# Moving twelve weight loads from the sync queue to GpSimd's queue

## The chip, the core and the metric

The kernel runs on one core of one Trainium2 chip. The metric is the device time of one execution in microseconds (us), the median of several runs. One more execution is recorded by the hardware profiler; its trace is what the tables and rows below are from.

## What is computed

Three layers follow each other. First comes a windowed attention over 2 x 8 heads of 576 positions. Its result, 1152 tokens of 512 numbers, goes through a layer of eight experts, each token to one of them. Last comes a dense layer with a gated activation.

```python
x = attention(q, k, v)                      # window of 64; (1152, 512), float32
e = argmax(x @ w_gate); g = softmax(x @ w_gate)[e]
y = g * (relu(x @ w1[e]) @ w2[e])           # 8 experts, 512 -> 1024 -> 512, float32 weights
h = y @ w_in                                # 512 -> 2048
out = (h * clip(h + 3, 0, 6) / 6) @ w_out   # 2048 -> 512
```

The dense layer's weights `w_in` and `w_out` arrive as float64. The chip reads them as pairs of 32-bit words and the kernel turns them into float32 itself.

## The kernel before

**Stages.** Up to about 67 us of the trace the kernel does attention. From about 67 to 235 us it does the experts ("the expert stage" below), from 235 us to the end the dense layer. The weights of an expert or of the dense layer are cut into units of 256 hidden columns. A unit has two halves of 512 KB, one for each matrix. An expert half is loaded into a `raw` buffer (six of them) by `weights_in` (lines 280 and 283), then split into a high and a low part for three-pass products: ScalarE casts the high part (line 267), VectorE subtracts to get the low part (line 272), both into `wt` buffers (eight). Two of the experts are small ("tiny") and use the `raw` halves without a split. TensorE's products of the weights are line 253.

**The float64 pieces.** A dense unit is converted in four pieces of 512 KB (`conv64`). Each is loaded into a `raw64` buffer, of which there are three (shown as `raw` in the trace), from `w_in` at line 196 or from `w_out` at line 199. Then follow one operation on ScalarE (line 206) and six on VectorE (lines 210, 214, 221, 227, 230 and 236), which go through the scratch tiles `c64` and `t64` (two each, shown as `c` and `t`). The last one, the add at line 236, makes the `raw64` buffer free. The pieces of the first three dense units (`NSC = 3`, twelve pieces) are worked on beside the experts: the float32 result is stored to a DRAM scratch by GpSimd (line 239) and read again for the dense stage at line 1134. The pieces of the later five units are converted in the dense stage and stay on the chip.

**What sets the order.** Each engine and each queue runs its instructions in the order in which they were written. That order is written by a small planner. It keeps an estimated clock for each engine (`est`; "D" stands for the DMA traffic, "P" for GpSimd), and a list of jobs sorted by due time. After every piece of hand-ordered work `fill(limit)` writes further operations of the jobs: one on "D" if it may start by `limit + 4.0`, one on any other engine only if it would end by `limit + 0.5`.

```python
def fill(limit):
    if live[0]:
        while advance(lambda j, e, t, c: t <= limit + SLACK_D if e == "D" else t + c <= limit + SLACK):
            pass
```

A conversion piece is such a job: load, absolute value on ScalarE, six operations on VectorE, and a store on GpSimd where the piece belongs to the first three units (`m is None`). Its load may be written only when the planner knows when a `raw64` buffer is free. GpSimd's own queue holds, in the expert stage, ten gathers of token rows (line 805) and the twelve stores.

In the listing below the sync queue is `nc.sync` and GpSimd's queue `nc.gpsimd`. In the profile they are SPq and POOL or POOLq; DVE is VectorE, ACT is ScalarE, PE is TensorE.

Of the kernel before, what the change touches and what calls it, by code (L numbers as in the profile page):

```python
# [23 lines left out]
def tile_kernel(ctx, tc, q, k, v, w_gate, w1, w2, w_in, w_out, out, cap):  # L24
    nc = tc.nc
    B, H, S, D = q.shape
# [151 lines left out]
    NSC = 3  # L178
# [3 lines left out]
    w_out32 = w_out.bitcast(U32)  # L182
# [3 lines left out]
    def conv64(u, i, dst):  # L186

        box = {}  # L190

        def load():
            box["raw"] = raw = cv.tile([128, 2 * HW], U32, name="raw64", bufs=NR64)
            if i < 2:
                src = w_in32[256 * i : 256 * i + 256, 2 * FU * u : 2 * FU * u + 2 * FU]
                nc.sync.dma_start(raw.rearrange("p (c f) -> p c f", c=2), src.rearrange("(c p) f -> p c f", p=128))
            else:
                r0 = FU * u + 128 * (i - 2)
                nc.sync.dma_start(raw, w_out32[r0 : r0 + 128, :])
            w = raw.rearrange("p (n t) -> p n t", t=2)  # L200
            box["lo"], box["hi"] = w[:, :, 0], w[:, :, 1]

        def c_abs():
            box["c"] = cv.tile([128, HW], U32, name="c64", bufs=NC64)
            box["t"] = cv.tile([128, HW], F32, name="t64", bufs=NC64)
            nc.scalar.activation(box["c"].bitcast(F32), box["hi"].bitcast(F32), AF.Abs)  # L206

        def c_clamp():
            c = box["c"].bitcast(F32)
            nc.vector.tensor_scalar(out=c, in0=c, scalar1=TINY, scalar2=HUGE, op0=ALU.max, op1=ALU.min)  # L210

        def c_shift():
            c = box["c"]
            nc.vector.tensor_scalar(
                out=c, in0=c, scalar1=0x07FFFFFF, scalar2=3, op0=ALU.bitwise_and, op1=ALU.logical_shift_left
            )

        def a_join():
            d = dst()
            box["a"] = a = box["hi"].bitcast(F32) if d is None else d  # L220
            nc.vector.scalar_tensor_tensor(
                out=a.bitcast(U32), in0=box["hi"], scalar=0xC0000000, in1=box["c"],
                op0=ALU.bitwise_and, op1=ALU.bitwise_or,
            )

        def c_power():
            nc.vector.tensor_single_scalar(box["c"], box["a"].bitcast(U32), 0xFF800000, op=ALU.bitwise_and)

        def t_low():
            nc.vector.scalar_tensor_tensor(  # L230
                out=box["t"], in0=box["lo"], scalar=2.0 ** -52, in1=box["c"].bitcast(F32), op0=ALU.mult, op1=ALU.mult
            )

        def t_add():
            a, t = box["a"], box["t"]
            nc.vector.tensor_tensor(out=a if u >= NSC else t, in0=a, in1=t, op=ALU.add)

        def store():
            nc.gpsimd.dma_start(wd_dram[u][:, HW * i : HW * i + HW], box["t"])

        return load, c_abs, c_clamp, c_shift, a_join, c_power, t_low, t_add, store

    NR64, NC64 = 3, 2
# [83 lines left out]
    with ExitStack() as actx:  # L327
# [343 lines left out]
        for j in range(NJ):  # L671
            p = 10 * j + (PRIO["tail"] if j == NJ - 1 else 0)
# [44 lines left out]
        p = 10 * NE + PRIO["top"]  # L717
# [278 lines left out]
        p = -100  # L996
# [57 lines left out]
    for n, (small, b) in enumerate(TEAMS):  # L1054
        at_ = dict.fromkeys("abw", 0)
        order = ORDER[n]
        for c in order:
            f = at_[c]
# [23 lines left out]
    def spend(e, cost, ready=0.0):  # L1082
        est[e] = max(est[e], ready) + cost
        return est[e]
# [16 lines left out]
    r_raw, r_wt, r_64, r_ct = Ring(2 * NRAW), Ring(2 * NWT), Ring(NR64), Ring(NC64)  # L1101
# [16 lines left out]
    def take_raw(m, h):  # L1118
        r_raw.take()
        raw_t[m, h] = rawp.tile([128, HALF], F32, name="raw")  # L1120
# [26 lines left out]
    def conv_job(u, i, m=None):  # L1147
        h = i // 2
        ix = {}

        def dst():
            return None if m is None else raw_t[m, h][:, HW * (i % 2) : HW * (i % 2) + HW]

        load, c_abs, *mid, t_add, store = conv64(u, i, dst)

        def gate_load():
            a = 0.0 if m is None or (m, h) in raw_t else r_raw.free(raw_at[m, h])
            b = r_64.free()
            return None if a is None or b is None else max(a - 2.0, b)

        def run_load(e, fin):
            if m is not None and (m, h) not in raw_t:
                take_raw(m, h)
            ix["raw"] = r_64.take()
            load()
            return fin + 2.0

        def run_abs(e, fin):
            ix["ct"] = r_ct.take()
            c_abs()  # L1170
            return fin

        def plain(fn):
            def run(e, fin):
                fn()
                return fin + 0.13

            return run

        def run_add(e, fin):  # L1180
            t_add()
            r_64.rel[ix["raw"]] = fin
            if m is not None:
                r_ct.rel[ix["ct"]] = fin
                raw_ready[m, i] = fin + 0.2
            return fin + 0.2

        def run_store(e, fin):
            store()
            r_ct.rel[ix["ct"]] = fin + 2.0  # L1190
            stored[u, h] = stored.get((u, h), 0) + 1
            return fin

        now = lambda: 0.0
        ops = [({"D": 1.46}, gate_load, run_load), ({"A": 0.6}, r_ct.free, run_abs)]
        ops += [({"V": c}, now, plain(fn)) for c, fn in zip((0.34, 0.4, 0.62, 0.34, 0.62), mid)]
        ops.append(({"V": 0.62}, now, run_add))
        return ops + ([({"P": 1.1}, now, run_store)] if m is None else [])
# [32 lines left out]
    for m, (kind, s, u) in enumerate(units):  # L1231
        for i in range(NPC):
            if not whole(m):
                add_job(m + 0.1 * i, m, split_job(m, i))
            if kind == "d" and u >= NSC:
                add_job(m - AHEAD[1] + 0.1 * i, m, conv_job(u, i, m))
            elif kind == "d":
                add_job(m + ZDUE + 0.1 * i, m, conv_job(u, i))
        if kind == "e" or u < NSC:
            for h in range(2):  # L1240
                add_job(m - AHEAD[0] + 0.1 * h, m, load_job(m, h))
# [427 lines left out]
    def dense_again():  # L1669

        for t0 in range(0, NTOK, 512):
            n = min(512, NTOK - t0)
            acc = [bank("acc") for _ in range(n // 128)]
            for u in range(DFF // FU):
                halves = [wk.tile([128, 2, NC, 256], F32R, name="xT256", bufs=XTB) for _ in range(2)]
                halves = [x.rearrange("p a c f -> p a (c f)") for x in halves]
                for i in range(NPC):
                    r = wk.tile([128, HW], F32, name="xg", bufs=3)
                    if u < NSC:
                        nc.sync.dma_start(r, wd_dram[u][:, HW * i : HW * i + HW])  # L1680
                    else:
                        load, c_abs, *mid, t_add, _ = conv64(u, i, lambda: r)
                        for fn in (load, c_abs, *mid, t_add):
                            fn()
                    high, low = split_ops(halves[i // 2], r, i % 2)
                    high("A")
                    low()
# [302 lines left out]
```

## Time and profile before

| | |
|---|---|
| median of 3 runs | 446.98 us (444.02 to 447.99) |
| the profiled execution: time, span of its trace | 445.77 us, 444.1 us |
| TensorE busy | 408.7 us, 92% of the span |
| VectorE busy | 321.5 us, 72% |
| ScalarE busy | 225.2 us, 51% |
| GpSimd busy | 57.0 us, 13% |
| DMA traffic | 75.99 MB, mean 171 GB/s |
| mean granted clock of TensorE | 0.978 of full speed |

Busy shares are means over stages that have different limits, so each stage has to be read on its own. DMA share in the windows is the mean busy share of the core's 16 DMA engines; it can exceed 1 slightly.

### The profile page before, as it was taken

The page shows a single profiled execution, that of the slowest core. Times are in us where ns is not written, and L with a number is a line of the kernel's source. Part 1 is how long each engine was busy: PE and PEld are TensorE (multiplying, and loading weights), DVE is VectorE, ACT ScalarE, POOL GpSimd, SP SyncE. Part 2 cuts the span into 40 slices and gives each one's busy share as a digit, 9 for nine tenths or more (in the row PEclk, how much of TensorE's full clock was granted, in tenths as well). Part 3 has the DMA queues.
Part 4 walks back from the last instruction along what each step waited for, and adds up shares of the span by engine and source line. Part 5 has one row for each costly group of instructions (what it writes and reads, how often), then busy time and mean ns, then how long its engine had stood idle before and what let it go on. Part 6 is the DMA issues. An engine that isn't in the chain of part 4 may idle for free.

```text
span 444.1 us, 8559 instructions
## 1 busy us (share of the span) xinstructions
PE 408.7 (92%) x3055; PEld 347.8 (78%) x3055; DVE 321.5 (72%) x865; ACT 225.2 (51%) x494; POOL 57.0 (13%) x120
## 2 busy tenths in 40 slices
PE   7999888797798699999999999999999999999991
PEld 4877665595696699997889998888888888998981
DVE  2888967597799599989967999999999422222430
ACT  4776763552567586744668453455553222322330
POOL 8533403003002100210000000000000000110110
PEclk9999999999699889999999999999999999999997
DMA  9897958939996999939985323442410000110101
GB/s 173 195 226 174 307 193 267 359 126 286 373 376 194 354 311 318 289 96 345 368 295 181 99 90 100 138 124 70 139 50 0 1 0 0 49 47 1 47 27 52
DMA packets 68883, 75.99 MB, mean 171 GB/s; under 512 B 31104, under 2 KB 49536, under 8 KB 68832
## 3 DMA queue, kind: packets, MB, share of 16 engines
q1 hardware_dynamic: 66288, 67.13, 49.4%
q0 software_dynamic: 2544, 8.23, 5.2%
q8 instruction: 26, 0.43, 0.4%
q14 instruction: 25, 0.20, 0.1%
HBM read 67.49 MB, written 7.86 MB: 170 GB/s over the span
## 4 chain that ended last, share of the span: by engine, by line
PE 63%; DMA 14%; DVE 12%; ACT 5%; issue 3%; SPq 1%; POOL 0%; POOLq 0%; ACTq 0%; DVEq 0%
PE banks L253 55%; DMA raw<-in_moe_w_dram 7%; DVE wt L272 3%; DMA raw<-in_moe_w_out_dram 3%; PE banks L628 2%; PE banks L510 2%; DMA c<-x_dram,sidx 1%; ACT wt L267 1%; DMA v_sb<-in_v_dram 1%; DMA k_sb<-in_k_dram 1%; DVE neg L587 1%; PE banks L574 1%; PE banks L1470 1%; PE banks L610 1%; ACT pe L600 1%
## 5 line engine op out<-in xcount | busy, mean ns | idle before, releaser
L253 PE MATMUL banks<-x,wt 128*128 128x320 f32 (+3 forms) x576 | 107.1, 336 | 0.7 <-ACT x L1386 0.4
L253 PEld LDWEIGHTS banks<-x,wt 128*128 128x128 f32 x576 | 94.3, 188 | 10.9 <-DVE wt L272 0.8
L272 DVE TENSOR_TENSOR wt<-raw,wt 128x512 fp32r<-128x512 f32 x128 | 82.9, 685 | 17.6 <-ACT wt L267 17.2
L253 PE MATMUL banks<-wt,g 128*128 128x512 f32 x384 | 92.8, 390 | 0.0
L267 ACT CAST wt<-raw 128x512 fp32r<-128x512 f32 x128 | 74.6, 620 | 29.7 <-DMA raw<-in_moe_w_dram 20.9
L253 PEld LDWEIGHTS banks<-wt,g 128*128 128x128 f32 x384 | 71.6, 188 | 14.2
L1556 ACT ACTIVATE r<-banks,c_three 128x320 f32<-128x320 f32 (+3 forms) x48 | 27.9, 581 | 70.0 <-PE banks L253 70.0
L1559 DVE SCALAR_TENSOR_TENSOR gf<-r,banks 128x320 f32<-128x320 f32 (+3 forms) x48 | 26.5, 552 | 47.6 <-ACT r L1556 47.2
L253 PE MATMUL banks<-xT,wt 128*128 128x256 f32 (+2 forms) x288 | 38.5, 283 | 1.9 <-DVE wt L272 1.7
L253 PEld LDWEIGHTS banks<-xT,wt 128*128 128x128 f32 x288 | 34.9, 191 | 3.9 <-DVE wt L272 1.9
L253 PE MATMUL banks<-h,wt 128*128 128x256 f32 (+2 forms) x288 | 37.0, 279 | 0.0
L253 PEld LDWEIGHTS banks<-h,wt 128*128 128x128 f32 x288 | 34.7, 192 | 0.5 <-issue 0.5
L1562 ACT CAST g<-gf 128x320 fp32r<-128x320 f32 (+2 forms) x40 | 21.4, 535 | 21.1 <-DVE gf L1559 20.9
L253 PE MATMUL banks<-wt,xT 128*128 128x256 f32 x144 | 23.7, 315 | 7.3 <-ACT wt L267 7.1
L1565 DVE TENSOR_TENSOR g<-gf,g 128x320 fp32r<-128x320 f32 (+2 forms) x40 | 23.3, 583 | 9.5 <-ACT g L1562 9.1
L253 PEld LDWEIGHTS banks<-wt,xT 128*128 128x128 f32 x144 | 21.0, 213 | 9.8 <-ACT wt L267 8.4
L206 ACT ACTIVATE c<-raw 128x512 f32<-128x512 f32 x32 | 21.5, 674 | 10.5 <-DVE t L230 10.1
L1602 POOL DMA_INDIRECT out_dram<-raw,cidx x4 | 3.9, 987 | 166.9 <-issue 164.3
L253 PE MATMUL banks<-wt,h 128*128 128x512 f32 x72 | 20.7, 424 | 3.7 <-ACT h L1436 3.7
L587 DVE CUSTOM_DVE_ANT_0 neg<-banks,tmask 128x128 f32<-128x128 f32 x72 | 16.2, 285 | 9.2 <-PE banks L574 9.2
L600 ACT ACTIVATE pe<-neg,nmx 128x128 f32<-128x128 f32 x72 | 22.3, 392 | 0.1
L230 DVE SCALAR_TENSOR_TENSOR t<-raw,c 128x512 f32<-128x512 uint32 x32 | 22.0, 687 | 0.4
(285 smaller groups left out, 566.2 us busy)
## 6 DMA issues: line engine op xcount, KB each, us to landing
raw<-in_moe_w_dram SPq DMA_DIRECT2D x64, 512.0 KB, 6.0
raw<-in_moe_w_in_dram SPq DMA_DIRECT2D x16, 512.0 KB
raw<-in_moe_w_out_dram SPq DMA_DIRECT2D x16, 512.0 KB, 3.9
early<-in_moe_w_dram SPq DMA_DIRECT2D x8, 512.0 KB, 4.5
wd_dram<-t POOLq DMA_DIRECT2D x12, 256.0 KB, 6.2
raw<-wd_dram SPq DMA_DIRECT2D x6, 512.0 KB, 5.5
x_dram<-xt SPq DMA_DIRECT2D x9, 256.0 KB, 4.8
q_sb<-in_q_dram SPq DMA_DIRECT2D x8, 256.0 KB, 4.0
```

Of the source, the lines that this page charges most:

```text
L206: nc.scalar.activation(box["c"].bitcast(F32), box["hi"].bitcast(F32), AF.Abs)
L230: nc.vector.scalar_tensor_tensor(out=box["t"], in0=box["lo"], scalar=2.0 ** -52, in1=box["c"].bitcast(F32), op0=ALU.mult, op1=ALU.mult)
L253: nc.tensor.matmul(out, l, r, start=(start and n == 0), stop=(stop and n == len(pairs) - 1))
L267: nc.scalar.copy(hi, r)
L272: V.tensor_tensor(out=lo, in0=r, in1=hi.bitcast(F32), op=ALU.subtract)
L510: nc.tensor.transpose(pt[:, hp, :], t[:, 2 * hp : 2 * hp + 2, :].rearrange("p h d -> p (h d)"), ident)
L587: V.tensor_tensor_reduce(out=neg[:, hp, :], in0=box["sp", g][:, hp, :], in1=tmask[:, first, :], scale=-1.0, scalar=3.0e38, op0=ALU.add, op ...
L600: nc.scalar.activation(pe[:, hp, :], neg[:, hp, :], AF.Exp, bias=nmx[:, hp : hp + 1], scale=-1.0)
L1556: nc.scalar.activation(r, ph, AF.Relu, bias=c_three)
L1559: V.scalar_tensor_tensor(out=gf, in0=r, scalar=6.0, in1=ph, op0=ALU.min, op1=ALU.mult)
L1562: nc.scalar.copy(hi, gf)
L1565: V.tensor_tensor(out=lo, in0=gf, in1=hi.bitcast(F32), op=ALU.subtract)
```

## The change

The loads of the twelve pieces that are converted beside the experts are issued from GpSimd's queue. The pieces of the dense stage keep the sync queue. The planner's cost of such a load goes to GpSimd ("P", 1.1 us), and the DMA estimate still gets its 1.46 us behind it.

```diff
+        queue = nc.gpsimd if u < NSC else nc.sync
         def load():
...
-                nc.sync.dma_start(raw.rearrange("p (c f) -> p c f", c=2), src.rearrange("(c p) f -> p c f", p=128))
+                queue.dma_start(raw.rearrange("p (c f) -> p c f", c=2), src.rearrange("(c p) f -> p c f", p=128))
             else:
                 r0 = FU * u + 128 * (i - 2)
-                nc.sync.dma_start(raw, w_out32[r0 : r0 + 128, :])
+                queue.dma_start(raw, w_out32[r0 : r0 + 128, :])
...
             ix["raw"] = r_64.take()
             load()
-            return fin + 2.0
+            return (fin if m is not None else spend("D", 1.46, fin)) + 2.0
...
-        ops = [({"D": 1.46}, gate_load, run_load), ({"A": 0.6}, r_ct.free, run_abs)]
+        ops = [({"D": 1.46} if m is not None else {"P": 1.1}, gate_load, run_load), ({"A": 0.6}, r_ct.free, run_abs)]
```

## Rows read from the trace of the kernel before

**Rows 1.** The page: busy time, and the chain that ended last, by line.

```profile
PE 408.7 (92%) x3055; PEld 347.8 (78%) x3055; DVE 321.5 (72%) x865; ACT 225.2 (51%) x494; POOL 57.0 (13%) x120
...
PE banks L253 55%; DMA raw<-in_moe_w_dram 7%; DVE wt L272 3%; DMA raw<-in_moe_w_out_dram 3%; PE banks L628 2%; PE banks L510 2%; DMA c<-x_dram,sidx 1%; ACT wt L267 1%; DMA v_sb<-in_v_dram 1%; DMA k_sb<-in_k_dram 1%; DVE neg L587 1%; PE banks L574 1%; PE banks L1470 1%; PE banks L610 1%; ACT pe L600 1%
```

**Rows 2.** Windows by stage: length, busy times, granted clock, DMA share, GB/s.

```profile
67.00:235.00 168.00, 149.93 (x1153) 129.56 (x1151) 138.79 (x318) 98.02 (x213) 20.21 (x24) 0.96 0.88 291
235.00:330.00 95.00, 94.32 (x480) 82.18 (x481) 89.87 (x177) 49.03 (x91) 0.00 (x0) 1.00 0.37 111
...
76.00:88.00 12.00, 8.75 (x44) 6.09 (x44) 6.79 (x12) 6.34 (x14) 0.00 (x0) 1.00 1.06 362
88.00:153.00 65.00, 53.35 (x427) 47.14 (x425) 53.24 (x127) 35.23 (x77) 10.24 (x12) 0.94 0.86 283
153.00:190.00 37.00, 36.54 (x275) 34.62 (x276) 35.88 (x80) 28.21 (x60) 2.72 (x2) 0.92 0.94 307
190.00:235.00 45.00, 43.99 (x370) 37.23 (x368) 36.50 (x78) 24.80 (x57) 2.91 (x5) 1.00 0.82 276
```

**Rows 3.** Timeline of the sync queue: start, length, line, what it loads.

```profile
82.71 0.98 SPq L196 DMA_DIRECT2D raw<-in_moe_w_in_dram  x2
...
88.73 0.38 SPq L280 DMA_DIRECT2D raw<-in_moe_w_dram  x1
98.34 0.34 SPq L199 DMA_DIRECT2D raw<-in_moe_w_out_dram  x1
...
132.24 0.37 SPq L280 DMA_DIRECT2D raw<-in_moe_w_dram  x1
140.43 0.38 SPq L196 DMA_DIRECT2D raw<-in_moe_w_in_dram  x1
...
185.79 0.37 SPq L280 DMA_DIRECT2D raw<-in_moe_w_dram  x1
195.65 3.36 SPq L199 DMA_DIRECT2D raw<-in_moe_w_out_dram  x2
```

**Rows 4.** Windows around the gaps in rows 3; columns as in rows 2.

```profile
93.00:98.00 5.00, 5.00 (x47) 4.43 (x46) 4.86 (x13) 2.27 (x6) 0.00 (x0) 1.00 0.02 5
...
107.00:114.00 7.00, 0.88 (x8) 0.64 (x6) 1.74 (x5) 0.79 (x2) 0.19 (x1) 0.78 1.05 359
114.00:118.00 4.00, 3.85 (x18) 3.33 (x20) 3.87 (x8) 3.64 (x9) 0.00 (x0) 0.54 1.07 365
...
136.00:141.00 5.00, 4.75 (x34) 3.93 (x34) 4.68 (x10) 4.74 (x11) 0.30 (x1) 1.00 0.30 97
...
149.50:153.30 3.80, 0.05 (x2) 0.01 (x1) 1.21 (x4) 1.92 (x5) 0.00 (x0) 0.80 1.06 309
153.30:157.00 3.70, 3.70 (x11) 3.12 (x12) 3.70 (x9) 3.69 (x8) 0.00 (x0) 0.50 1.03 355
...
190.00:196.00 6.00, 6.00 (x55) 5.28 (x54) 5.70 (x16) 3.00 (x7) 0.09 (x1) 1.00 0.02 5
```

**Rows 5.** Timeline of ScalarE: in brackets the idle time before, and its releaser.

```profile
79.33 0.62 ACT L267 CAST wt<-raw 128x512 fp32r<-128x512 f32 x1 [2.32 <-DMA raw<-in_moe_w_dram]
...
113.48 2.23 ACT L267 CAST wt<-raw 128x512 fp32r<-128x512 f32 x4 [5.30 <-DMA raw<-in_moe_w_dram]
```

**Rows 6.** Groups by line, 67 to 235 us: busy, mean ns, idle before.

```profile
L805 POOL DMA_INDIRECT xg<-x_dram,sidx x10 | 12.0, 1198 | 34.5 <-PE banks L1306 31.9 <-issue 1.7 <-PE banks L1483 0.3
...
L206 ACT ACTIVATE c<-raw 128x512 f32<-128x512 f32 x12 | 8.1, 681 | 0.2 <-DVE top_f L1773 0.2
L239 POOL DMA_DIRECT2D wd_dram<-t x12 | 7.1, 590 | 98.3 <-DVE t L236 67.5 <-DVE ks L1734 24.0 <-ACT y L1456 6.6
```

**Rows 7.** DMA issues of the page: KB each, median us to landing.

```profile
wd_dram<-t POOLq DMA_DIRECT2D x12, 256.0 KB, 6.2
...
xg<-x_dram,sidx POOLq DMA_INDIRECT x10, 6.7
```

**Rows 8.** Timeline of GpSimd, the last of the three gathers before the experts.

```profile
73.31 1.27 POOL L805 DMA_INDIRECT xg<-x_dram,sidx  x1 [0.30 <-issue]
```

## The prediction

> **What bounds the kernel now.** I read the page first. TensorE is busy for 92% of the span, and on the chain that ended last it has most of the time, but a load of expert weights (`raw<-in_moe_w_dram`) stands there with 7% and VectorE's split with 3% [rows 1]. So the chain leaves TensorE for the DMA somewhere. The windows by stage say where [rows 2]: in the dense stage up to 330 us TensorE is busy for 94.3 of 95 us and nothing is to be had. In the expert stage, 67 to 235 us, it is busy for 149.9 of 168. Nearly all that is missing lies in one stretch: from 88 to 153 us it is busy for 53.35 of 65, so it idles 11.65 us there; from 153 to 190 it idles 0.46 and from 190 to 235 us 1.0.
>
> The next view is the timeline of the sync queue [rows 3]. Three times a load of a float64 piece (line 199 or 196) goes out long after the load written before it: 98.34 after 88.73, 140.43 after 132.24, 195.65 after 185.79. The piece needs a `raw64` buffer, and that comes free with the add of an earlier piece on VectorE. Everything behind it on the queue waits too, and that is expert halves. The DMA engines run dry meanwhile: their share is 0.02 from 93 to 98 us, 0.30 from 136 to 141, 0.02 from 190 to 196 [rows 4]. Before the first of these gaps, from 76 to 88 us, the share was 1.06 at 362 GB/s [rows 2]. So it isn't a lack of bandwidth; the traffic is held back by the order of one queue.
>
> TensorE feels it later. From 107 to 114 us it is busy for 0.88 of 7 us, from 149.5 to 153.3 us for 0.05 of 3.8 [rows 4]. The first idle stretch ends when ScalarE casts an expert half at 113.48, after 5.30 us of waiting for that half's DMA [rows 5], which had been queued behind the piece that left at 98.34. TensorE then works with a granted clock of 0.54 from 114 to 118 us and of 0.50 from 153.3 to 157 [rows 4]: after an idle stretch it is granted mostly the lower of its two levels, 1.2 instead of 2.4 GHz. That costs about 3.85 x 0.46 = 1.8 and 3.70 x 0.50 = 1.85 us of work. The third gap costs hardly anything, since TensorE loses only 1.0 us from 190 us on.
>
> **The change, part by part.**
>
> *Removed: twelve loads from the sync queue.* Each took 0.34 to 0.38 us to issue [rows 3], which the queue's idle time hides. What counts is the wait in front of them, which leaves with them. Expert halves then go out as soon as their own `raw` buffers are free. What is late next? Three limits for the stretch of 65 us. TensorE could gain its idle time and the first slow clock, 11.65 + 1.8 = 13.5 us. The DMA moves 283 x 65 = 18.4 MB, which takes 50.8 us at 362 GB/s, so it could give up 14 us. VectorE has 53.24 us of work there; in the next stretch, where nothing was held back, it was busy for 35.88 of 37 us (0.970), and in the dense stage for 89.87 of 95 (0.946) [rows 2]. At 0.970 its work needs 54.9 us and at 0.946 56.3. VectorE is therefore the tightest, and the gain is 8.7 to 10.1 us; I take the middle, 9.4. The third gap adds at most the 1.0 us that TensorE idles after it. The second slow clock (1.85 us) I count only in the lower end of the range, because from 153 us on VectorE is full anyway.
>
> *Added: twelve loads on GpSimd's queue.* No load of this kind is in the trace. The nearest are the stores, 0.590 us of GpSimd each, and the gathers, 1.198 [rows 6]. I take 0.6 for the four-kilobyte rows of `w_out`, which are 128 as in a store, and 1.2 for the pieces of `w_in` with twice as many. Both kinds are six, so it is 6 x 0.6 + 6 x 1.2 = 10.8 us (7 to 14 at the ends) on an engine that is busy for 20.2 of 168 us [rows 2]. That is hidden, and with no cover at all it would be 10.8 us late. From GpSimd a store of 256 KB takes 6.2 us to land and a gather 6.7 [rows 7]; a load of 512 KB should take 6 to 8.
>
> *Added: waits on GpSimd's queue.* The wait for the `raw64` buffer moves there. Behind it stand stores of other pieces and gathers. But the load of piece n+3 and the store of piece n wait for the same add, so the store loses at most one issue, 1.2 us. The gathers have their own long waits there now (one of 31.9 us for TensorE's transposes [rows 6]) and go out a team of experts ahead, except the last one. Cost: 0, at most 1.2 us for that last gather.
>
> *Moved: the first three loads.* Their buffers are free from the start, and GpSimd is free once the third gather is out, at 73.31 + 1.27 = 74.6 us [rows 8]. In the code these loads now follow those gathers as soon as the planner's limit reaches them. Before, they stood behind expert halves and the first two went out at 82.71 us [rows 3]. So 3 x 0.524 MB come into a stretch in which the DMA runs at 362 GB/s, which is 4.3 us of traffic. If all of it goes ahead of expert halves that are awaited, TensorE is 4.3 us late; if none does, 0. That the halves are awaited there is seen at 79.33, where ScalarE's cast waited 2.32 us for one [rows 5]. The two queues share the engines, so I take half, 2.2 us. In exchange VectorE may do a piece in its idle time from 76 to 88 us (5.2 us); I count nothing for it.
>
> *Moved in the code's order.* A load on "P" is written when it would end by `limit + 0.5`, before it could be up to 4 us ahead. On GpSimd's queue only the order counts, and what stands before it is short. Cost 0, with the rival below as its bound.
>
> The Trainium skill's page "DMA: Bandwidth & Descriptors", section "Issuing engines are not separate DMA queues", speaks against the change: transfers from any engine end up on the same 16 DMA engines and interleave, and issuing from several only saves the time of issue. By that the time would stay at 447. The gaps of rows 4 speak for another reading here: the engines stood empty while a queue waited.
>
> Sum: 9.4 + 1.0 - 2.2 = 8.2 us less. The profiled execution took 445.77 us, so it would take 437.6. It lies 1.2 us below the median of the runs shown, 446.98; against that median, which I forecast, it is 438.8.
>
> **The rivals.**
>
> *VectorE or ScalarE takes the place of the wait, about no change.* VectorE was busy for 4.86 of 5 us just while the DMA was empty [rows 4]: it did pieces one after another. If it does so again, and now earlier, the splits of the expert halves stand behind them, the `raw` buffers come free late, and the sync queue waits for those instead. For this: 53.24 of 65 us is not much slack. Against: in the gaps there was no expert half to split at all. Of the 9.4 us perhaps a third would be left, less the 2.2: 1 us, 446.
>
> *ScalarE stands at the absolute value (line 206), slower.* The planner lets it come 1.1 + 1.46 + 2.0 = 4.6 us after the load's turn. If a load takes 6.7 us to land like a gather [rows 7], after 1.2 of issue, ScalarE waits up to 3.3 us for each of the nine later pieces, 30 us in all, and the casts of expert halves stand behind it. ScalarE has 70 of 168 us idle [rows 2], so I let half reach TensorE: 15 - 8.2 = 7 us slower, 454. It decides from the point at which a load lands more than 4.6 us after its buffer is free and VectorE isn't late itself. Against it: twelve such operations waited 0.2 us in all before [rows 6], and they need the store of an earlier piece, which lands after 6.2 us, as late as the load.
>
> The skill has a rule that would make this worse: "SBUF — State Buffer", section "SBUF: two separate sides", says that GpSimd can't write descriptors while VectorE runs an operation in a two-port mode, and that switching to the other queues avoids it. No row here shows such a stall: the stores took 0.59 us each beside a full VectorE.
>
> *It doesn't do what it says.* GpSimd's queue is as much in order as the other one. If loads stand there behind stores (their idle time before is 98.3 us [rows 6]), the pieces come as late as now, the scratch is read late, and the dense stage starts late. Expert halves still flow, so it ends about where it was: 445 to 450, taken as 447.
>
> **How the numbers follow.** The forecast has 0.60, and all of its own range (434 to 442.5) is faster by over 1%; 1% of 447 is 4.5 us, about what a measurement of this kernel can tell from no change. The first rival has 0.18 (no change), the slower one 0.14, the last 0.08, half of it no change and half slower. The forecast gets most because the empty DMA and its cause are seen directly; the rest is large because every engine's order is written anew by the planner. So faster 0.62 (with 0.02 of the first rival), same 0.20, slower 0.18. Low end: all limits at their best, 10.1 + 1.0 + 1.85 and nothing for the first loads, 13 us: 434, and 1 below it for the spread of the runs. High end: no change, and 1.5 us above it.
>
> **What would show it.** Right: from 88 us on no load of an expert half stands behind a piece; the DMA share has no window near 0; the idle time of TensorE at 107 and 149 us and the low clock after it are gone; the dense stage starts about 8 us earlier and is as long as before. Wrong: casts or line 206 on ScalarE that wait for DMA, a late first product at 82 to 88 us, waits of the sync queue for splits (line 272) that grow by as much as those for pieces shrink, or VectorE with new idle time before splits.

## The result and the profile after

The median went from 447.49 us (444.02 to 448.96, four runs) to 441.52 us (440.29 to 443.19, four runs). The ratio is 0.9887, 95% interval 0.9849 to 0.9925: 1.1% faster, 6.0 us by the medians. The profiled execution took 440.54 us (span 438.8), 5.2 us less than that of before; its forecast was 437.6. The changed kernel was timed again later: 440.26 us, ratio 0.9879 (0.9841 to 0.9918). All line numbers from 192 on are two higher than before.

First the page, busy times and chain, to be held against [rows 1].

```profile
PE 407.9 (93%) x3055; PEld 345.7 (79%) x3055; DVE 321.2 (73%) x864; ACT 225.0 (51%) x495; POOL 65.1 (15%) x132
...
PE banks L255 36%; DMA raw<-in_moe_w_in_dram 1%; DVE raw L223 1%; DVE t L232 1%; DVE raw L238 1%; DVE g L1567 1%; DVE c L212 1%; DVE wt L274 1%; DMA wd_dram<-t 1%; DVE gf L1561 0%; DVE c L229 0%; DVE c L216 0%; DVE part L1595 0%; POOL out_dram L1604 0%; ACT c L208 0%
```

This chain can be followed back only to 233.14 us, so its shares say nothing about the expert stage and can't be held against the 7% of before. At its start stand a store to the scratch (`wd_dram<-t`), a load of a float64 piece and the conversion of pieces. What became of the expert stage is seen in the windows. The windows by stage and around the old gaps, with the columns of [rows 2] and [rows 4]:

```profile
76.00:88.00 12.00, 9.54 (x52) 6.62 (x50) 8.42 (x15) 6.44 (x14) 0.00 (x0) 1.00 1.05 362
88.00:153.00 65.00, 63.03 (x506) 56.30 (x506) 59.70 (x141) 44.99 (x100) 11.52 (x14) 1.00 0.96 326
153.00:190.00 37.00, 36.49 (x308) 33.60 (x307) 33.75 (x79) 21.99 (x49) 6.19 (x7) 1.00 0.88 289
190.00:235.00 45.00, 43.93 (x336) 38.50 (x335) 38.97 (x76) 26.91 (x58) 4.03 (x7) 1.00 0.62 213
235.00:330.00 95.00, 89.67 (x423) 75.29 (x422) 84.79 (x167) 46.41 (x84) 0.00 (x0) 0.98 0.39 117
...
93.00:98.00 5.00, 5.00 (x49) 4.47 (x48) 5.00 (x14) 3.79 (x9) 0.60 (x1) 1.00 0.76 223
107.00:114.00 7.00, 6.43 (x48) 5.16 (x47) 6.90 (x14) 5.65 (x12) 0.00 (x0) 1.00 1.04 381
149.50:153.30 3.80, 3.54 (x24) 3.28 (x25) 3.80 (x9) 3.15 (x7) 0.00 (x0) 1.00 1.06 371
190.00:196.00 6.00, 5.62 (x45) 4.87 (x45) 5.93 (x12) 4.26 (x10) 1.15 (x2) 1.00 0.97 277
```

The stretch from 88 to 153 us is as forecast: TensorE is busy for 63.03 us instead of 53.35, the DMA share is 0.96 instead of 0.86, both idle stretches and the low clock after them are gone. But the row of 235 to 330 us has turned: 89.67 of 95 us instead of 94.32. The timeline of TensorE in the changed kernel tells where (in brackets the idle time before, and its releaser):

```profile
221.16 7.01 PE L255 MATMUL banks<-x,wt 128*128 128x320 f32 x46 [0.36 <-ACT x L1388]
...
260.26 3.48 PE L255 MATMUL banks<-wt,g 128*128 128x512 f32 x14 [1.23 <-DVE wt L274]
266.50 5.04 PE L255 MATMUL banks<-x,wt 128*128 128x320 f32 x20 [2.18 <-DVE wt L274]
```

The same mark in the kernel before, TensorE's first long group in the dense layer (in both kernels two products stand 0.93 us ahead of it), and GpSimd's last store:

```profile
235.84 7.01 PE L253 MATMUL banks<-x,wt 128*128 128x320 f32 x46 [0.36 <-ACT x L1386]
...
221.89 0.54 POOL L239 DMA_DIRECT2D wd_dram<-t  x1 [6.61 <-ACT y L1456]
```

So the dense layer starts 14.68 us earlier (235.84 - 221.16), and the span ends only 5.3 us earlier (444.1 - 438.8): 9.4 us come back behind this first dense group. The chain of the changed kernel, in order of time (start, length, what), shows the beginning of it:

```profile
233.14 2.33 DMA wd_dram<-t
235.97 5.62 DMA raw<-in_moe_w_in_dram
241.61 0.67 ACT c L208
```

VectorE's timeline has the wait that this makes:

```profile
242.31 0.43 DVE L212 TENSOR_SCALAR c<-c 128x512 f32<-128x512 f32 x1 [7.81 <-ACT c L208]
```

GpSimd's and the sync queue's timelines belong to it, with the third gather for [rows 8]:

```profile
72.62 1.27 POOL L807 DMA_INDIRECT xg<-x_dram,sidx  x1 [0.30 <-issue]
73.89 1.55 POOL L198 DMA_DIRECT2D raw<-in_moe_w_in_dram  x2
...
233.14 0.54 POOL L241 DMA_DIRECT2D wd_dram<-t  x1 [16.55 <-DVE t L238]
```

```profile
205.99 29.94 SPq L1136 DMA_DIRECT2D raw<-wd_dram  x6
235.97 0.94 SPq L198 DMA_DIRECT2D raw<-in_moe_w_in_dram  x2
```

The twelfth piece is stored at 233.14, 12 us after the first dense group; before it was stored at 221.89, 14 us ahead of it. The last of the six reloads (line 1136) waits for that store, and the pieces of the dense stage stand behind it on the sync queue. ScalarE stands for the first of them until 241.61, and VectorE behind it for 7.81 us. From then on VectorE converts without a pause until 272 us, and TensorE waits for the split at 260.26 and 266.50.

### The profile page after: what moved, and what is told of

It reads as the page before. It is cut to its first block, busy times and chain, and to the rows that moved or that the text cites. A ratio compares the mean times of both kernels' runs of the same rounds, so it can differ in the third digit from the quotient of the medians.

```text
span 438.8 us, 8564 instructions
## 1 busy us (share of the span) xinstructions
PE 407.9 (93%) x3055; PEld 345.7 (79%) x3055; DVE 321.2 (73%) x864; ACT 225.0 (51%) x495; POOL 65.1 (15%) x132
## 5 line engine op out<-in xcount | busy, mean ns | idle before, releaser
L255 PE MATMUL banks<-x,wt 128*128 128x320 f32 (+3 forms) x576 | 108.7, 340 | 2.6 <-DVE wt L274 2.2
L255 PEld LDWEIGHTS banks<-x,wt 128*128 128x128 f32 x576 | 95.8, 191 | 12.8 <-DVE wt L274 2.7
L255 PE MATMUL banks<-wt,g 128*128 128x512 f32 x384 | 94.3, 392 | 3.1 <-DVE wt L274 1.2
L255 PE MATMUL banks<-wt,xT 128*128 128x256 f32 x144 | 21.7, 293 | 1.3 <-DVE wt L274 0.8
L223 DVE SCALAR_TENSOR_TENSOR raw<-raw,c 128x512 uint32<-128x512 uint32 x32 | 22.0, 688 | 0.5
L255 PEld LDWEIGHTS banks<-wt,xT 128*128 128x128 f32 x144 | 18.6, 190 | 3.9 <-DVE wt L274 2.3
```

What stands on the lines that cost most here:

```text
L223: nc.vector.scalar_tensor_tensor(out=a.bitcast(U32), in0=box["hi"], scalar=0xC0000000, in1=box["c"], op0=ALU.bitwise_and, op1=ALU.bitwise_or,)
L255: nc.tensor.matmul(out, l, r, start=(start and n == 0), stop=(stop and n == len(pairs) - 1))
```

## The experiments

The change has two halves, the queue and the planner's costs, and the planner writes every engine's order anew. So the first two kernels separate them, and the next try the end of the chain.

**The queue alone.** The planner is left as it was; PE, VectorE and ScalarE run exactly the order of before. As an edit of the changed kernel:

```diff
-            return (fin if m is not None else spend("D", 1.46, fin)) + 2.0
+            return fin + 2.0
...
-        ops = [({"D": 1.46} if m is not None else {"P": 1.1}, gate_load, run_load), ({"A": 0.6}, r_ct.free, run_abs)]
+        ops = [({"D": 1.46}, gate_load, run_load), ({"A": 0.6}, r_ct.free, run_abs)]
```

> The twelve loads go out from GpSimd's queue, but the planner's costs stay as in the kernel before, so PE, VectorE and ScalarE run the very order of before. Theory (the wait in front of the loads was what cost): the three gaps of the DMA go, and the gain is at least that of the change, 5 to 10 us: 437 to 443 us. Rival (the new order of the engines brought the gain): within 1% of before, 445 to 449.

Measured: 438.63 us (437.31 to 441.89) against 445.25, ratio 0.9856 (0.982 to 0.9892). With no other order on any engine the gain is there, so the wait in front of the pieces was the cause. Its windows, from 88 us and in the dense stage:

```profile
88.00:153.00 65.00, 60.28 (x483) 53.07 (x484) 61.96 (x145) 43.23 (x95) 14.45 (x18) 1.00 0.95 319
...
235.00:330.00 95.00, 94.75 (x468) 81.56 (x467) 90.46 (x177) 46.27 (x83) 0.00 (x0) 1.00 0.32 95
```

VectorE is at 61.96 of 65 (0.953), where the prediction had set its limit (0.946 to 0.970). TensorE's idle time there falls from 11.65 to 4.72 us, and in the three windows in which the DMA had run dry (93 to 98, 136 to 141, 190 to 196 us) its share is 0.75, 0.99 and 1.00. The dense stage is full, as before.

**The planner alone.** The loads stay on the sync queue; PE, VectorE and ScalarE run exactly the order of the changed kernel.

```diff
-        queue = nc.gpsimd if u < NSC else nc.sync
+        queue = nc.sync
```

> The planner's costs as in the changed kernel, so PE, VectorE and ScalarE run the order of after, but all loads stay on the sync queue. Theory (queue): expert halves stand behind pieces again, with gaps of the DMA as before, 446 to 455 us. Rival (order): as fast as the changed kernel, 440 to 443.

Measured: 439.91 us (438.55 to 441.05), ratio 0.9875 (0.9846 to 0.9904). My theory that the gaps would stay fell. The planner's new entry writes a load only if it would end by `limit + 0.5`; before it could be 4 us ahead. So more expert halves stand in front of it. Sync queue and windows of this kernel:

```profile
170.79 0.37 SPq L282 DMA_DIRECT2D raw<-in_moe_w_dram  x1
180.61 2.97 SPq L198 DMA_DIRECT2D raw<-in_moe_w_in_dram  x2
```

```profile
88.00:153.00 65.00, 63.51 (x515) 57.04 (x514) 59.92 (x141) 45.34 (x101) 8.21 (x10) 1.00 0.99 330
...
170.00:181.00 11.00, 11.00 (x98) 10.10 (x97) 10.19 (x24) 6.49 (x16) 0.12 (x1) 1.00 0.33 98
```

Two waits for a `raw64` buffer of the old length are left: 7.0 us before the load at 90.51, behind which the next expert half leaves at 94.01 (in the changed kernel, where no piece stands in front of it on this queue, at 93.98), and 9.4 us before 180.61. During the second TensorE is busy for all of 11 us. Either half removes the gaps that hurt. On this chip the queue alone takes 6.6 us off, the planner alone 5.3, both together 6.0 in the first result, so the gains don't add. This kernel has the new order of every engine besides the later loads; which of the two brought its gain was not taken apart.

**The reloads on GpSimd too.** In the changed kernel the sixth reload held the sync queue until 235.9 us. Here the six reloads leave from GpSimd.

```diff
-                nc.sync.dma_start(t, wd_dram[u][:, HALF * h : HALF * h + HALF])
+                nc.gpsimd.dma_start(t, wd_dram[u][:, HALF * h : HALF * h + HALF])
```

> The changed kernel with the six loads that read the scratch again (line 1136) on GpSimd's queue too; the engines' order is that of after. Theory (in the changed kernel the sixth of them holds up the first float64 pieces of the dense stage on the sync queue until 236 us, and ScalarE, VectorE and then TensorE stand for them from 234 to 270 us): those waits go, 4 to 7 us less than the changed kernel, 434 to 438. Rival (the dense stage is bound by VectorE there anyway): no change, 440 to 443.

Measured: 439.80 us (437.09 to 441.61), ratio 0.9864 (0.9827 to 0.9901), so no clear gain over the changed kernel; 4 to 7 us were expected. Two dense pieces now leave at 208 us, and the absolute value at 235.13 waits for nothing. ScalarE's next cast takes the wait over:

```profile
243.49 0.62 ACT L269 CAST wt<-raw 128x512 fp32r<-128x512 f32 x1 [7.24 <-DMA raw<-wd_dram]
```

GpSimd in the same kernel, the last store and the reload that waits for it to land:

```profile
234.40 0.55 POOL L241 DMA_DIRECT2D wd_dram<-t  x1 [16.54 <-DVE t L238]
239.45 0.54 POOL L1136 DMA_DIRECT2D raw<-wd_dram  x1 [4.51 <-DMA wd_dram<-t]
```

So freeing the sync queue is not enough. What is waited for now is the twelfth piece itself; that an earlier twelfth piece would save the time isn't shown by this run, and the run on its due time below speaks against it.

**All pieces on GpSimd.** The dense stage's twenty loads move too.

```diff
-        queue = nc.gpsimd if u < NSC else nc.sync
+        queue = nc.gpsimd
```

> The changed kernel with the twenty pieces of the dense stage on GpSimd's queue as well. There they stand behind the store of the last piece (233 us) instead of behind the load that reads it again. Theory: the first of them comes only some 2 to 3 us earlier than in the changed kernel, so 1 to 3 us less, 438 to 441. Rival (loads from GpSimd cost more than from the sync queue): slower than the changed kernel, over 443.

Measured: 441.36 us (440.33 to 442.07), ratio 0.9907 (0.988 to 0.9934). This can't be told apart from the changed kernel, and the rival's over 443 us didn't come; TensorE is busy for 89.22 us from 235 to 330. The loads now stand behind the last store (230.84) instead of the sixth reload.

**The changed kernel again**, beside the next three.

> The changed kernel once more, beside the next three on the same chip: 439 to 443 us.

Measured: 440.26 us (438.6 to 442.29) against 445.4.

**The twelve pieces due earlier.** The due time of the twelve scratch pieces is moved forward in the planner's list, so that it finishes them ahead of more of the dense stage's work.

```diff
-    ZDUE = 3
+    ZDUE = -2
```

> The changed kernel with an earlier due time for the twelve pieces (ZDUE -2 instead of 3). VectorE's order for the first eleven stays; the twelfth piece is done after 1 of the dense stage's four VectorE chunks instead of after all 4. Theory (the dense stage is late because the twelfth piece is joined, stored and read again too late in VectorE's order): its store leaves before 225 us instead of at 233, the waits from 234 to 270 us shrink, and the time is 2 to 5 us under the changed kernel's. Rival (VectorE has too much work there in any order): same as the changed kernel.

Measured: 439.59 us (438.49 to 441.65), ratio 0.988 (0.9846 to 0.9914), the same as the changed kernel, where 2 to 5 us less were expected. The last store comes at 225.65 instead of 233.14, and the small waits of the dense stage give way to a single one of the same size:

```profile
235.91 5.45 PE L255 MATMUL banks<-x,wt 128*128 128x320 f32 x20 [4.72 <-DVE wt L274]
```

VectorE's wait has only moved, it is no shorter (8.26 us instead of 7.81):

```profile
234.83 0.43 DVE L212 TENSOR_SCALAR c<-c 128x512 f32<-128x512 f32 x1 [8.26 <-ACT c L208]
```

**GpSimd's operations up to 1 us ahead** instead of 0.5, so that loads and stores of pieces are written earlier.

```diff
-            while advance(lambda j, e, t, c: t <= limit + SLACK_D if e == "D" else t + c <= limit + SLACK):
+            while advance(lambda j, e, t, c: t <= limit + SLACK_D if e == "D" else t + c <= limit + (1.0 if e == "P" else SLACK)):
```

> The changed kernel in which the planner may write GpSimd's operations up to 1.0 us after its limit instead of 0.5. By the order that it writes, the twelfth piece is done before any chunk of the dense stage, as in the kernel before, and the first pieces stay early. Theory: the expert stage ends at 221 to 227 us as in the changed kernel and in the one with the old order, and the dense stage loses nothing: 432 to 438 us, the fastest so far. Rival (the early pieces cost the experts what they give the dense stage): 438 to 443.

Measured: 440.84 us (438.9 to 441.97), ratio 0.9897 (0.9863 to 0.993); expected was less. The dense stage is full again (94.53 of 95 us). In exchange the experts wait, and the first dense group comes at 229.36 us instead of 221.16:

```profile
127.57 3.14 PE L255 MATMUL banks<-xT,wt 128*128 128x256 f32 x12 [1.70 <-ACT wt L269]
...
196.31 2.91 PE L255 MATMUL banks<-wt,h 128*128 128x512 f32 x6 [2.00 <-ACT h L1438]
```

**The queue alone, without the first three loads.** As the first experiment, but the first three stay in their old place on the sync queue.

```diff
-        queue = nc.gpsimd if u < NSC else nc.sync
+        queue = nc.gpsimd if u < NSC and (u, i) > (0, 2) else nc.sync
```

> The kernel of the queue alone (old order of the engines), but with the first three loads left on the sync queue, behind the expert halves as before. By the prediction's term (three loads ahead of awaited expert halves cost 2.2 us) it is about 2 us faster than the queue alone. Rival (they cost nothing, since nothing that TensorE waits for is delayed): the same as the queue alone, within 1 us.

Measured: 436.64 us (434.35 to 437.93), ratio 0.9786 (0.9753 to 0.9819). On the same chip the changed kernel took 438.6 to 442.29. Then this kernel ran once more beside the first experiment's.

> The loads on GpSimd's queue with every engine's order as before, once more, beside the two below on one chip. Theory (the first three loads cost 2 to 3 us when they go ahead of awaited expert halves): 438 to 440. Rival (the first three cost nothing, the difference seen between two calls was the chips'): the same time as the next kernel, within 1 us, at 436 to 438.

> As the last, but the first three loads stay on the sync queue, in their old place behind expert halves. Theory: 2 to 3 us below the kernel above, 435 to 437. Rival: within 1 us of it.

Measured: 440.25 us (438.92 to 441.53, ratio 0.987, 0.9836 to 0.9904) with all twelve moved, 437.38 us (436.68 to 438.99, ratio 0.9816, 0.9781 to 0.9852) with nine. By the medians on one chip the three loads cost 2.9 us in the old order; the slowest run with nine (438.99) is about the fastest with twelve (438.92). ScalarE with all twelve moved:

```profile
88.67 0.62 ACT L269 CAST wt<-raw 128x512 fp32r<-128x512 f32 x1 [5.46 <-DMA raw<-in_moe_w_dram]
89.19 0.58 ACT L468 COPY c<-banks 128x512 f32<-128x512 f32 x1
```

and with nine, the same two:

```profile
85.59 0.62 ACT L269 CAST wt<-raw 128x512 fp32r<-128x512 f32 x1
...
86.84 0.59 ACT L468 COPY c<-banks 128x512 f32<-128x512 f32 x1 [0.63 <-PE banks L255]
```

A cast waits 5.46 us for its expert half (3.01 us in the first experiment's profile), and the copy behind it, which TensorE needs, comes 2.35 us later than with nine. TensorE with all twelve moved:

```profile
89.82 1.12 PE L1405 MATMUL banks<-ident,c 128*128 128x128 f32 x4 [3.76 <-ACT c L468]
```

From 88 to 93 us, around the end of this wait, its granted clock is 0.52, so nearly all of that time the lower of its two levels. In the first experiment's execution, the same program, it idled 1.30 us in this place and the clock stayed at 1.00; that span, 436.3 us, is no longer than those with nine (436.2 and 436.5). So the cost differs between executions, and part of it is the slow clock.

**The same in the changed kernel.** First with its order kept and only the queue of the three loads put back, then with queue and cost put back, so that the planner writes a third order.

> The changed kernel with its own order, but the first three loads on the sync queue. If the first three cost the changed kernel as much as they cost the old order, 2 us below the changed kernel, 438. If its dense stage takes back what the expert stage gains, as I think from its trace, no difference: 440 to 441. Rival (in the new order the planner writes these loads earlier, so on the sync queue they stand ahead of more expert halves): 441 to 443.

> The whole change, queue and planner costs, applied to nine of the twelve loads; the first three keep the sync queue and the old cost, so the planner may write them early and behind expert halves again. Every engine's order is a third one. If going ahead of awaited halves is what the first three cost in the changed kernel too, 437 to 438.5. If the order that the planner writes for VectorE is what decides, the time follows from where it puts the twelfth piece's join, and it may lie anywhere from 437 to 442; the first dense product near 221 us with a dense stage of less than 91 of 95 us, or near 227 with a full one, would show it.

Measured: 440.04 us (437.82 to 442.17, ratio 0.9881, 0.984 to 0.9923) and 440.23 us (439.48 to 442.44, ratio 0.9889, 0.9841 to 0.9937): no difference from the changed kernel. Neither is the test that I meant. In the first the planner's order has the three loads early on the sync queue too, from 73.18 us on, ahead of the awaited halves. In the second three other pieces took the free buffers, from GpSimd at 73.80 to 75.87, and the three that stayed went out at 89.55, 102.51 and 123.53. What the second shows is that another order of the same rule has the same pattern. TensorE in it:

```profile
221.53 3.64 PE L255 MATMUL banks<-x,wt 128*128 128x320 f32 x23 [0.36 <-ACT x L1388]
...
260.73 3.47 PE L255 MATMUL banks<-wt,g 128*128 128x512 f32 x14 [1.24 <-DVE wt L274]
266.97 3.51 PE L255 MATMUL banks<-x,wt 128*128 128x320 f32 x20 [2.19 <-DVE wt L274]
```

Early start and waits for splits are those of the changed kernel; its last store is at 233.52.

## Why the prediction was right, and which steps were not

**What bounds the kernel.** Right, and shown: moving the queue of twelve loads with every compute engine's order held takes 5.8 to 6.6 us off (two measurements), and with it the empty windows of [rows 4] and more than half of TensorE's idle time from 88 to 153 us go. "Nearly all" was too much for that stretch, though: of the 18.07 us that TensorE idles from 67 to 235 us, 11.65 lie in it and 4.95 ahead of it, from 67 to 88 us, where the changed kernel still idles 4.61. The Trainium skill's page "DMA: Bandwidth & Descriptors", section "Issuing engines are not separate DMA queues", would have allowed only the time of issue. The trace agrees that both queues fill the same engines (share 0.96 over 65 us), but not that only issue time is saved: an issue took 0.34 to 0.38 us beside work [rows 3], and the gain is some 6 us, because a load that waits holds those behind it.

**9.4 + 1.0 for the wait.** Right in kind, high in size. The cleanest measure is nine loads moved with the order held, where the first three stay out of it: 8.8 and 8.7 us off the medians (445.40 - 436.64, 446.04 - 437.38), not 10.4. The limit taken, VectorE, was at 0.953 in the first experiment. It was a limit of that order only: with the new one TensorE does more in the same stretch (63.03 us) beside less work of VectorE (59.70, 0.918). The second slow clock, which the sum left out, did go: from 153 to 190 us the granted clock is 1.00 instead of 0.92, with as much of TensorE's time in use.

**2.2 for the first three loads.** Borne out in the old order (2.9 us by the medians, a part of it slow clock). In the changed kernel the trace shows nothing like it: ScalarE does two absolute values in that place, and its next cast comes at 90.99 us without a wait. No run took the three loads alone out of the way there, so for that order it stays open.

**10.8 us on GpSimd.** It was 7.8: the loads' groups by line are

```profile
L198 POOL DMA_DIRECT2D raw<-in_moe_w_in_dram x6 | 4.4, 743 | 24.6 <-DVE cp L1811 15.6 <-DVE t L238 7.6 <-DVE top_f L1815 1.4
L201 POOL DMA_DIRECT2D raw<-in_moe_w_out_dram x6 | 3.4, 572 | 31.0 <-DVE h L1368 23.0 <-DVE t L238 8.0
```

The gather was the wrong neighbour for `w_in`: 0.74 us, not 1.2. It stayed hidden. The landing, 6 to 8 us, was right; the page's issues of the changed kernel:

```profile
raw<-in_moe_w_in_dram POOLq DMA_DIRECT2D x6, 512.0 KB, 7.6
raw<-in_moe_w_out_dram POOLq DMA_DIRECT2D x6, 512.0 KB, 7.1
```

**"Moved in the code's order. Cost 0."** This step failed, and with it "starts about 8 us earlier and is as long as before". From the third gather (72.62 instead of 73.31 [rows 8]) the experts are 14.68 - 0.69 = 14.0 us shorter, where I had 8.2; and the part behind the first dense group is 438.8 - 221.16 = 217.6 us instead of 208.3. With the order held (the first experiment, third gather at 72.78) that group began at 226.62 and the rest took 436.3 - 226.62 = 209.7. So in these profiles the planner's new order makes the experts 5.3 us shorter and what follows 8.0 us longer; neither was in the sum.

Of the 8.0 us, 3.2 are TensorE's busy time behind the first dense group (202.22 instead of 199.02) and 4.8 its idle time. About 1.6 of the 3.2 are clock: from 260 to 280 us the granted clock was 0.91 in the changed kernel and 1.00 with nine of twelve, which has the same two waits and a busy time of 200.67 us. The idle time follows the 7.81 us that VectorE stands still early in the dense layer.

In the total the two effects nearly cancel: the medians of the whole change (ratios 0.9887, 0.9879) and of the queue alone (0.9856, 0.987) don't separate. The forecast of 438.8 was 2.7 us low and inside its range. For the queue it was right for its reason: 8.7 for the wait less 2.9 for the first three loads is 5.8 us, where I had 8.2 and the whole change gave 6.0. That the order's term came out near 0 in the total is luck: it is the difference of two effects that the prediction had not seen.

Why the planner's estimates put the twelfth piece there, and whether its place is what costs the dense layer its 8 us, is not settled. Three attempts to have both ends (reloads elsewhere, an earlier twelfth piece, GpSimd's work earlier) each showed a wait in another place. Of the kernels of the experiments, those whose first dense group begins at 222.4 us or earlier lose some 5 to 6 us to waits in the first 60 us of the dense layer; those where it begins at 226.6 us or later lose 0.5 us or less from 235 to 330 us.

**The rivals.** *VectorE takes the wait's place:* not so. The sign that I had named did come up in part, though. The sync queue's waits, 67 to 235 us (total us, times, longest), before:

```profile
SPq L280 <- DVE wt L272: 18.5, 11, 6.1
SPq L283 <- DVE wt L272: 17.4, 12, 5.1
SPq L199 <- DVE c L214: 11.7, 2, 9.7
SPq L199 <- DVE ks L1734: 9.0, 1, 9.0
SPq L196 <- DVE t L236: 7.9, 2, 7.7
...
SPq L199 <- DVE t L236: 6.3, 2, 3.7
```

and after:

```profile
SPq L285 <- DVE wt L274: 28.3, 17, 5.2
SPq L282 <- DVE wt L274: 27.7, 15, 10.1
```

The waits for splits grew from 35.9 to 56.0 us while the 34.9 for pieces left this queue. TensorE, busy for 63.03 of 65 us from 88 us on, doesn't feel them: a load that waits for a split waits until a `raw` buffer of the experts is free, and the DMA share in that stretch is 0.96. A queue's waiting time alone was a poor sign. *ScalarE at the absolute value:* not in the expert stage, where these twelve waited 1.3 us in all, for TensorE. *It doesn't do what it says:* its wait for loads behind stores didn't come, but its end did in part: the scratch is written late. It came from the new order and not from GpSimd's queue: with the loads back on the sync queue (the planner alone) the last store leaves at 234.18, as late. The Trainium skill's page "SBUF — State Buffer", section "SBUF: two separate sides", says that GpSimd can't write descriptors beside a VectorE operation in a two-port mode. The time of issue shows no mark of it here: the loads took 0.57 and 0.74 us on average while VectorE was busy for 59.70 of 65 us. Which of its operations ran in such a mode no run tells.

**The best version** is the queue alone with nine loads and the old planner: ratios 0.9786 and 0.9816, 3.6 us under the changed kernel on the same chip (440.26 - 436.64).

## What to carry to other kernels

Where the DMA engines run empty while loads are queued, look for the load in front that waits for a buffer. Here giving it another queue took 6.6 us off, writing it later (with the new order that this brought) 5.3, and both together 6.0: the gains don't add. Where a planner writes the order from costs, price the change with the order held and the new order as two terms, and follow the last piece of side work through to whoever reads it. Loads whose buffers are free from the start have nothing to gain from another queue, and ahead of awaited weights they cost 2.9 us here.

## What the runs showed of the hardware

A load of 512 KB from GpSimd took 0.572 us to issue in 128 rows of 4 KB and 0.743 us in 256 rows of 2 KB; a store of 256 KB in 128 rows took 0.574 us. In these three forms the issue followed the rows and hardly the bytes. And a wait of 2.18 us at 266.50 was followed by a lower clock in the changed kernel's execution (0.91 from 260 to 280 us; its group of 20 products took 5.04 us; 0.91 again in its second profile), while after 2.19 us at 266.97 the same group took 3.51 us with nine of twelve, at 1.00: whether the lower of the two levels, 1.2 instead of 2.4 GHz, was granted didn't follow from the length of the wait alone.
